# Banded attention and a gated feed-forward on one core: the convolution's weights converted at the start, and the weight chunks converted with two VectorE instructions fewer

## The chip, the cores and the metric

The kernel runs on one core of one Trainium2 chip. The time is the device time of one execution in microseconds (us); before the change it was 523.57 us, the median of three runs (522.38 to 523.83). Five engines work side by side, each through its own list of instructions in a fixed order: TensorE (PE in the profile, its weight loads PEld), VectorE (DVE), ScalarE (ACT), GpSimd (POOL) and SyncE (SP), which here only starts transfers. An instruction at the head of a list that waits holds up everything behind it on that engine.

## What is computed

The reference, cut to what matters:

```python
scores = scale * np.matmul(q, k.transpose(0, 1, 3, 2))     # 8 batches, 8 heads, 576 positions, 64 wide
scores = np.where(masks, scores, -1e9)                      # heads 0-3: last 32 positions; 4-7: every 4th of the last 128
attn = softmax(scores)
x = np.matmul(attn, v)                                      # heads side by side: (8, 576, 512)
h = np.maximum(x @ w_in, 0.0)                               # 512 -> 1024
conv_out = sum(conv_w[k] * shifted(h, k - 1) for k in range(3))
out = (h * sigmoid(conv_out)) @ w_out                       # 1024 -> 512
```

`w_in`, `conv_w` and `w_out` arrive as 64-bit floats, read by the kernel as pairs of 32-bit integers, a low and a high word.

## The kernel before

The matrix products of the feed-forward part are made from pairs: every operand is a high part (rounded to the format `F32R`) plus a low part (what rounding left), and three products (high times high, high times low, low times high) are added in PSUM. So each weight has to be turned from two integer words into such a pair before TensorE can use it, and each attention output `x` too: ScalarE casts the PSUM tile to `x0a`, TensorE subtracts that from the PSUM tile with a matrix `minus` (line 334), and ScalarE casts what is left to `x0b` (line 337).

The work is in tasks. For each of the 8 batches there are 4 attention chains (two heads each: scores on TensorE at line 255, mask and maximum on VectorE at 266 and 268, the exponentials on ScalarE at 275, reciprocal, scaling and a transpose on VectorE at 288, 289 and 291, the values on TensorE at 307), and one expert chain: first product (367), rectifier on ScalarE (374), the convolution's taps, the gate and its split (385 to 396), second product (412), and the store. A planner (`Planner.order`) gets each task with an engine, a cost and a due time from a table (`DUE`), simulates the engines and buffers, and so fixes the order of instructions on every engine. In front of the first products TensorE gets dummy products with the matrix `eye` (`fill`, line 525), as many as fit in what the planner takes for its idle time between 5 and 31.5 us. There are 82 of them, in fixed places of TensorE's order, each a 128x512 product that nothing reads.

There is one PSUM buffer for attention (`att`), two buffers for raw weights (`raw_128` and `raw_129` in the listings), one scratch tile `t`, and two tiles `pt` for transposed probabilities. The weights come in eight chunks of 1 MB, four of `w_in` (converted to tiles `wi`) and four of `w_out` (tiles `wo`). Each chunk takes these steps (lines of the kernel before):

- SP starts the load into `raw` (470);
- ScalarE writes the absolute value of the high words to `t` (476);
- VectorE clamps `t` (477), shifts and masks its bits (479), and puts sign and exponent's top bit back (482): now `t` holds the weight, cut to the bits that `F32R` keeps;
- ScalarE casts `t` to the high part (484);
- VectorE shifts the low words (485) and joins to them the rest of the high words (487), takes the scale from `t` (489), and multiplies both to the low part (491). None of these four waits for ScalarE's cast.

In the order of their conversion, the first chunk goes to `wi_67` (high) and `wi_71` (low), the second to `wi_68` and `wi_72`, the third to `wi_66` and `wi_70`, the fourth to `wi_65` and `wi_69`. The two raw buffers alternate, so the load of the third chunk waits until the first one's last reader is done.

The convolution's 3 x 1024 weights are 24 numbers for each partition (`few_weights`). Their load stands in SP's list behind a dozen others (445); one ScalarE instruction (447) and six on VectorE (448 to 457) make them, as tasks of the planner, and VectorE reads the result `conv_sb` first at line 379.

At the very start, ahead of all tasks, ScalarE starts the load of the mask (497), copies half of the mask table (507 and 509), and makes `minus` and `eye` (499 and 500). TensorE's dummy products need `eye`.

Of the kernel before, what the change touches and what calls it, by code (L numbers as in the profile page):

```python
# [185 lines left out]
def attn_moe(ctx: ExitStack, tc: tile.TileContext, qk_p, qk_d, v_p, v_d, w_in, w_out, conv, mask, out):  # L186
    nc = tc.nc
# [47 lines left out]
    xs = {}  # L235

    def attention(b, p):
# [10 lines left out]
        def scores():  # L248
# [19 lines left out]
        last = plan.add("DVE", 0.755, soft + 0.5, lambda: nc.vector.tensor_reduce(  # L268
            out=m.t, in_=flat(), axis=AX.X, op=ALU.max, negate=slotwise), [last], [s, m])
# [166 lines left out]
    def few_weights(src, due):  # L436

        u, t = few
        low, high = (few_raw[:, :, i] for i in range(2))
        ui, ti = u.bitcast(I32), t.bitcast(I32)  # L440

        def step(run, after, engine="DVE"):
            return plan.add(engine, 0.2, due, run, [after])
# [3 lines left out]
        last = step(lambda: nc.scalar.activation(out=u, in_=high.bitcast(F32), func=AF.Abs), last, "ACT")  # L447
        last = step(lambda: nc.vector.tensor_scalar(out=u, in0=u, scalar1=2.0 ** -15, scalar2=None, op0=ALU.max), last)
        last = step(lambda: nc.vector.tensor_scalar(
            out=ti, in0=ui, scalar1=3, scalar2=0x3fffffff, op0=ALU.logical_shift_left, op1=ALU.bitwise_and), last)  # L450
        last = step(lambda: nc.vector.scalar_tensor_tensor(
            out=ti, in0=high, scalar=-0x40000000, in1=ti, op0=ALU.bitwise_and, op1=ALU.bitwise_or), last)
        last = step(lambda: nc.vector.tensor_scalar(
            out=ui, in0=ti, scalar1=-0x800000, scalar2=None, op0=ALU.bitwise_and), last)
        last = step(lambda: nc.vector.scalar_tensor_tensor(
            out=u, in0=low.bitcast(U32), scalar=2.0 ** -52, in1=u, op0=ALU.mult, op1=ALU.mult), last)
        return step(lambda: nc.vector.tensor_tensor(
            out=conv_sb.rearrange("p t c -> p (t c)"), in0=t, in1=u, op=ALU.add), last)

    def weights(src, due, fetch, hi, lo):  # L460
# [8 lines left out]
        bits = lambda x: x().bitcast(I32)  # L469
        load = plan.add("SP", 3.0, fetch, lambda: nc.sync.dma_start(  # L470
# [124 lines left out]
```

## Time and profile before

| | |
|---|---|
| time, median of three runs | 523.57 us (522.38 to 523.83) |
| the profiled execution | 520.62 us, of which the span from first to last instruction is 518.8 us |
| TensorE busy | 502.6 us (97%) |
| VectorE busy | 389.4 us (75%) |
| ScalarE busy | 303.9 us (59%) |
| granted TensorE clock | 0.999 |

A row of the timeline reads: start (us from the span's start), duration, engine, line, operation, output tile and input tile, shapes, count; in square brackets the engine's idle time ahead of it and what ended that. A row of the windows reads: stretch, its length, then the busy time and number of instructions of PE, PEld, DVE, ACT and POOL, the granted clock, the busy share of the DMA engines and GB/s. Names are of tiles, without their numbers in the timeline and with them in the listings of the order.

### The profile page before, as it was taken

The numbers are of one execution on the slowest core, as the hardware profiler recorded it, in microseconds if no ns is written. First come the engines' busy times: TensorE is split into PE (matmuls) and PEld (weight loads), VectorE is DVE, ScalarE is ACT, GpSimd is POOL, SyncE is SP. The second block draws the span as 40 slices with busy tenths as digits, with TensorE's granted clock in tenths as the row PEclk, the third lists the DMA queues.
The fourth block names the chain that finished last, engine by engine and source line by source line (L and its number), as shares of the span: only waits on it lengthen the run. The fifth ranks groups of instructions, "written<-read, shape, count | busy, mean of one in ns | idle before, by whom it ended". The sixth has DMA issues, their size and how long they took to land.

```text
span 518.8 us, 16673 instructions
## 1 busy us (share of the span) xinstructions
PE 502.6 (97%) x7542; PEld 438.9 (85%) x7542; DVE 389.4 (75%) x552; ACT 303.9 (59%) x624; POOL 1.4 (0%) x27
## 2 busy tenths in 40 slices
PE   5999999999999899999999999999989999999996
PEld 3578999999778898799878997899967899889985
DVE  4999999999986899739970599739989379418800
ACT  5968989748433677158741676448732388327710
POOL 1000000000000000000000000000000000000000
PEclk9999999999999999999999999999999999999999
DMA  7867452211255320413132114321244200110021
GB/s 280 304 200 273 161 158 99 68 52 58 89 178 173 105 80 21 150 52 93 52 103 89 52 48 126 125 82 52 93 119 131 74 1 1 42 42 1 0 62 41
DMA packets 16550, 50.98 MB, mean 98 GB/s; under 512 B 2016, under 2 KB 3168, under 8 KB 15456
## 3 DMA queue, kind: packets, MB, share of 16 engines
q1 hardware_dynamic: 16336, 49.84, 28.7%
q8 instruction: 59, 0.97, 0.8%
q10 hardware_dynamic: 144, 0.08, 0.1%
q14 instruction: 11, 0.09, 0.1%
HBM read 40.48 MB, written 9.44 MB: 96 GB/s over the span
## 4 chain that ended last, share of the span: by engine, by line
PE 86%; DVE 5%; ACT 4%; DMA 4%; issue 1%; ACTq 0%
PE nn L412 37%; PE mm L367 34%; PE att L307 6%; PE att L255 5%; DMA qk<-in_qk_d_dram 2%; PE nn L367 2%; PE nn L525 1%; ACT c L390 1%; ACT L390 1%; DMA c<-in_mask_dram 1%; DMA v<-in_v_p_dram 1%; DVE s L289 1%; DVE pt L291 1%; PE att L334 1%; ACT h L374 0%
## 5 line engine op out<-in xcount | busy, mean ns | idle before, releaser
L412 PE MATMUL nn<-wo,g 128*128 128x512 f32 (+1 forms) x960 | 210.8, 374 | 0.0
L412 PEld LDWEIGHTS nn<-wo,g 128*128 128x128 f32 x960 | 164.6, 188 | 32.0 <-ACT out L422 0.4
L379 DVE SCALAR_TENSOR_TENSOR c<-h,conv_sb,c 128x576 f32<-128x576 f32 x128 | 103.1, 813 | 44.3 <-ACT c L385 43.2
L374 ACT ACTIVATE h<-mm 128x288 f32<-128x288 f32 x120 | 48.3, 407 | 38.3 <-PE mm L367 38.2
L422 ACT COPY out<-nn 128x512 f32<-128x512 f32 (+1 forms) x40 | 21.7, 543 | 62.9 <-PE nn L412 59.0
L367 PE MATMUL mm<-x6a,wi 128*128 128x288 f32 x192 | 54.5, 298 | 0.2 <-ACT h L374 0.2
L392 DVE TENSOR_TENSOR c<-c,h 128x576 f32<-128x576 f32 x64 | 47.6, 755 | 6.8 <-ACT c L390 6.0
L394 ACT CAST g<-c 128x576 fp32r<-128x576 f32 x64 | 42.6, 672 | 17.3 <-DVE c L392 17.2
L385 ACT ACTIVATE c<-h,conv_sb 128x576 f32<-128x576 f32 x64 | 49.6, 777 | 3.7 <-DVE g L396 2.2
L390 ACT ACTIVATE c<-c 128x576 f32<-128x576 f32 x64 | 43.2, 684 | 12.4 <-DVE c L379 11.6
L396 DVE TENSOR_TENSOR g<-c,g 128x576 fp32r<-128x576 f32 x64 | 47.7, 755 | 2.4 <-ACT g L394 1.4
L255 PEld LDWEIGHTS att<-qk 64*32 64x32 f32 x2304 | 26.6, 108 | 18.4 <-issue 5.7
L255 PE MATMUL att<-qk 64*32 64x64 f32 x2304 | 32.2, 229 | 9.7 <-DMA qk<-in_qk_p_dram 5.4
L307 PEld LDWEIGHTS att<-pt,v 32*64 32x64 f32 x2624 | 31.1, 130 | 12.1 <-issue 4.9
L367 PE MATMUL mm<-x3a,wi 128*128 128x288 f32 x144 | 40.8, 299 | 0.2 <-ACT h L374 0.2
L367 PE MATMUL mm<-x2a,wi 128*128 128x288 f32 x144 | 40.8, 299 | 0.0
L367 PE MATMUL mm<-x1a,wi 128*128 128x288 f32 x144 | 40.3, 296 | 0.0
L367 PEld LDWEIGHTS mm<-x6a,wi 128*128 128x128 f32 x192 | 36.1, 188 | 1.0 <-ACT h L374 0.4
L367 PE MATMUL mm<-x5a,wi 128*128 128x288 f32 x128 | 36.4, 299 | 0.2 <-ACT h L374 0.2
L307 PE MATMUL att<-pt,v 32*64 32x64 f32 (+1 forms) x2624 | 34.6, 230 | 1.5 <-ACT x1b L337 1.1
L367 PE MATMUL mm<-x0a,wi 128*128 128x288 f32 x112 | 31.7, 300 | 0.0
L367 PE MATMUL mm<-x6b,wi 128*128 128x288 f32 x96 | 28.4, 296 | 0.0
(122 smaller groups left out, 797.7 us busy)
## 6 DMA issues: line engine op xcount, KB each, us to landing
qk<-in_qk_p_dram SPq DMA_DIRECT2D x16, 592.0 KB, 4.2
qk<-in_qk_d_dram SPq DMA_DIRECT2D x16, 592.0 KB, 4.2
out_dram<-out SPq DMA_DIRECT2D x28, 256.0 KB, 2.2
v<-in_v_d_dram SPq DMA_DIRECT2D x16, 384.0 KB, 3.6
v<-in_v_p_dram SPq DMA_DIRECT2D x16, 384.0 KB, 3.5
raw<-in_w_in_dram SPq DMA_DIRECT2D x4, 1024.0 KB, 6.4
raw<-in_w_out_dram SPq DMA_DIRECT2D x4, 1024.0 KB, 6.6
out_dram<-out SPq DMA_DIRECT2D x16, 128.0 KB, 2.0
```

Of the source, the lines that this page charges most:

```text
L255: nc.tensor.matmul(sc.t[quad * 32:quad * 32 + 32, o:o + W], qk.t[hd * 64:hd * 64 + 64, q0:q0 + 32], qk.t[hd * 64:hd * 64 + 64, S + q0:S + ...
L307: nc.tensor.matmul(tv.t[hd * 64:hd * 64 + 64, o:o + hi - lo], v.t[quad * 32:quad * 32 + 32, i, hd * 64:hd * 64 + 64], pt.t[quad * 32:quad ...
L367: nc.tensor.matmul(ps.t[:, 0:HALF], wi[jw][fc // 2][:, fc % 2, k], x[k].t[jx][:, hf * HALF:hf * HALF + HALF], start=(k == 0 and i == 0), s ...
L374: relu.append(plan.add("ACT", 0.4, due + 1.6 * u + 1.6, lambda fc=fc, hf=hf, ps=ps: nc.scalar.activation(out=h[fc].t[:, 1 + hf * HALF:1 + ...
L379: nc.vector.scalar_tensor_tensor(out=c[fc].t, in0=h[fc].t[:, k:S + k], scalar=conv_sb[:, k, fc:fc + 1], in1=c[fc].t, op0=ALU.mult, op1=ALU ...
L385: t = plan.add("ACT", 0.777, d, lambda fc=fc: nc.scalar.activation(out=c[fc].t, in_=h[fc].t[:, 1:S + 1], func=AF.Copy, scale=conv_sb[:, 1, ...
L390: t = plan.add("ACT", 0.686, d + 1.0, lambda fc=fc: nc.scalar.activation(out=c[fc].t, in_=c[fc].t, func=AF.Sigmoid), [t], [c[fc]], "sigmoid")
L392: t = plan.add("DVE", 0.755, d + 1.5, lambda fc=fc: nc.vector.tensor_tensor(out=c[fc].t, in0=c[fc].t, in1=h[fc].t[:, 1:S + 1], op=ALU.mult ...
L394: hi = plan.add("ACT", 0.675, d + 2.0, lambda fc=fc: nc.scalar.copy(out=half(fc, 0), in_=c[fc].t), [t, *(done[fc] if odd else [])], [c[fc] ...
L396: lo = plan.add("DVE", 0.755, d + 2.5, lambda fc=fc: nc.vector.tensor_tensor(out=half(fc, 1), in0=c[fc].t, in1=half(fc, 0).bitcast(F32), o ...
L412: nc.tensor.matmul(ps.t[:, 0:n], g[k // 2].t[:, k % 2, jg, c0:c0 + 128], w.rearrange("p h c -> p (h c)") if hf is None else w[:, hf], star ...
L422: last = plan.add("ACT", 0.582 if hf is None else 0.37, out_due + 8 * cost * (u + 1), lambda ps=ps, o=o, n=n: nc.scalar.copy(out=o.t[:, 0: ...
```

## The change

It has two parts, and the planner is given the same tasks at the same costs in both, so that its order stays as it was; some tasks now do nothing, and some do something else.

**The convolution's weights.** Their load moves from SP's list to ScalarE's, right behind that of the mask. Their seven instructions leave their places in the order; they are issued by the task of the very first maximum (`greatest`), behind its reduction. The one on ScalarE reads only the load, and there it is placed as soon as ScalarE's own start-up list allows.

**The weight chunks.** The third VectorE step keeps eight more bits of the high word (mask `0x3ffffff8` for `0x3ffff000`). The two steps on the low words do nothing any more. A new step shifts the low words right by 29 and joins them to `t`, so that `raw` holds the weight as a float32 of 24 bits (line 502 of the kernel after). ScalarE's cast of `t` still makes the high part (500), and the low part is now a subtraction, that float32 minus the high part (484), issued by whichever of the two tasks comes second. The task of the cast now counts as a user of the raw buffer. The diff, cut to this:

```diff
+        def greatest():
+            nc.vector.tensor_reduce(out=m.t, in_=flat(), axis=AX.X, op=ALU.max, negate=slotwise)
+            while early:
+                early.pop()()
...
-        last = plan.add("SP", 0.1, due - 2.0, lambda: nc.sync.dma_start(
-            out=few_raw, in_=src.bitcast(I32).rearrange("p (n t) -> p n t", t=2)))
-        last = step(lambda: nc.scalar.activation(out=u, in_=high.bitcast(F32), func=AF.Abs), last, "ACT")
...
+        nc.scalar.dma_start(out=few_raw, in_=src.bitcast(I32).rearrange("p (n t) -> p n t", t=2))
+
+        def steps():
+            nc.scalar.activation(out=u, in_=high.bitcast(F32), func=AF.Abs)
+            nc.vector.tensor_scalar(out=u, in0=u, scalar1=2.0 ** -15, scalar2=None, op0=ALU.max)
...
+        early.append(steps)
+        last = plan.add("SP", 0.1, due - 2.0, lambda: None)
+        for engine in ["ACT"] + 6 * ["DVE"]:
+            last = plan.add(engine, 0.2, due, lambda: None, [last])
...
+        def both(first=None):
+
+            if first:
+                first()
+            come.append(raw.t)
+            if len(come) == 2:
+                nc.vector.tensor_tensor(out=lo, in0=shaped(lw(), lo), in1=hi.bitcast(F32), op=ALU.subtract)
...
-            out=bits(t), in0=bits(t), scalar1=3, scalar2=0x3ffff000,
+            out=bits(t), in0=bits(t), scalar1=3, scalar2=0x3ffffff8,
...
-        high = plan.add("ACT", 1.14, due, lambda: nc.scalar.copy(out=hi, in_=shaped(t(), hi)), [top], [tb])
-        left = step(0.69, [load], lambda: nc.vector.tensor_scalar(
-            out=bits(lw), in0=bits(lw), scalar1=9, scalar2=None, op0=ALU.logical_shift_right))
-        left = step(1.22, [left], lambda: nc.vector.scalar_tensor_tensor(
-            out=bits(lw), in0=bits(hw), scalar=23, in1=bits(lw), op0=ALU.logical_shift_left, op1=ALU.bitwise_or))
-        last = step(0.69, [top, left], lambda: nc.vector.tensor_scalar(
-            out=bits(hw), in0=bits(t), scalar1=-0x800000, scalar2=None, op0=ALU.bitwise_and))
-        return [high, plan.add("DVE", 1.22, due, lambda: nc.vector.scalar_tensor_tensor(
-            out=lo, in0=shaped(lw().bitcast(U32), lo), scalar=2.0 ** -43, in1=shaped(hw(), lo),
-            op0=ALU.mult, op1=ALU.mult), [last], [raw])]
+        high = plan.add("ACT", 1.14, due, lambda: both(lambda: nc.scalar.copy(out=hi, in_=shaped(t(), hi))), [top], [tb, raw])
+        left = step(1.22, [step(0.69, [load], lambda: None)], lambda: None)
+        last = step(0.69, [top, left], lambda: nc.vector.scalar_tensor_tensor(
+            out=bits(lw), in0=bits(lw), scalar=29, in1=bits(t), op0=ALU.logical_shift_right, op1=ALU.bitwise_or))
+        return [high, plan.add("DVE", 1.22, due, both, [last], [raw])]
```

TensorE's order is the same before and after. Three places show what moved on the others. Lines of the kernel after are larger by 2 to 11 than those before for the same instruction.

ScalarE's list at its start, before (`c_123` is the raw mask, `pt_94` holds the unit matrix, `m_88` the first maximum):

```order
L497 DMA c_123<-in_mask_dram 128x320
L507 ACT_TABLE_LOAD
L507 COPY mask_sb<-c_123 128x576
L509 COPY mask_sb<-c_123 128x64
L509 COPY mask_sb<-c_123 128x128
L499 ACTIVATE minus<-pt_94 128x128
L500 CAST eye<-pt_94 128x128
L271 ACTIVATE m_88<-m_88 128x9
```

and after (`few_raw` is the raw convolution weights):

```order
L508 DMA c_123<-in_mask_dram 128x320
L446 DMA few_raw<-in_conv_dram 128x48
L518 ACT_TABLE_LOAD
L518 COPY mask_sb<-c_123 128x576
L449 ACTIVATE few_78<-few_raw 128x24
L520 COPY mask_sb<-c_123 128x64
L520 COPY mask_sb<-c_123 128x128
L510 ACTIVATE minus<-pt_94 128x128
L511 CAST eye<-pt_94 128x128
L276 ACTIVATE m_88<-m_88 128x9
```

The instruction that reads the convolution's weights stands behind the first copy of the mask, with two copies, `minus` and `eye` behind it.

VectorE's list around the first chunk's end, before (`s` and `z` belong to the attention tasks, `pt_95` to the second pair of heads):

```order
L482 SCALAR_TENSOR_TENSOR t_130<-raw_128,t_130 128x1024
L288 RECIPROCAL z_91<-z_91 128x9
L289 TENSOR_TENSOR s_85<-s_85,z_91 128x9x64
L489 TENSOR_SCALAR raw_128<-t_130 128x1024
L491 SCALAR_TENSOR_TENSOR wi_71<-raw_128 128x1024
L291 STREAM_TRANSPOSE pt_95<-s_87 128x576
L288 RECIPROCAL z_92<-z_92 128x9
L289 TENSOR_TENSOR s_86<-s_86,z_92 128x9x64
L485 TENSOR_SCALAR raw_129<-raw_129 128x1024
L487 SCALAR_TENSOR_TENSOR raw_129<-raw_129 128x1024
L477 TENSOR_SCALAR t_130<-t_130 128x1024
```

and after:

```order
L498 SCALAR_TENSOR_TENSOR t_130<-raw_128,t_130 128x1024
L293 RECIPROCAL z_91<-z_91 128x9
L294 TENSOR_TENSOR s_85<-s_85,z_91 128x9x64
L502 SCALAR_TENSOR_TENSOR raw_128<-raw_128,t_130 128x1024
L296 STREAM_TRANSPOSE pt_95<-s_87 128x576
L293 RECIPROCAL z_92<-z_92 128x9
L294 TENSOR_TENSOR s_86<-s_86,z_92 128x9x64
L484 TENSOR_TENSOR wi_71<-raw_128,wi_67 128x1024
L493 TENSOR_SCALAR t_130<-t_130 128x1024
```

The first chunk's last instruction moved behind the next transpose, reciprocal and scaling, and it now reads `wi_67`, which ScalarE's cast writes.

VectorE's list around the fourth chunk's end, before:

```order
L482 SCALAR_TENSOR_TENSOR t_130<-raw_129,t_130 128x1024
L489 TENSOR_SCALAR raw_129<-t_130 128x1024
L491 SCALAR_TENSOR_TENSOR wi_69<-raw_129 128x1024
L288 RECIPROCAL z_91<-z_91 128x9
L289 TENSOR_TENSOR s_85<-s_85,z_91 128x9x64
L291 STREAM_TRANSPOSE pt_94<-s_85 128x576
L266 TENSOR_TENSOR s_86<-att_131,mask_sb 128x9x64
L268 TENSOR_REDUCE m_89<-s_86 128x9
```

and after:

```order
L498 SCALAR_TENSOR_TENSOR t_130<-raw_129,t_130 128x1024
L502 SCALAR_TENSOR_TENSOR raw_129<-raw_129,t_130 128x1024
L484 TENSOR_TENSOR wi_69<-raw_129,wi_65 128x1024
L293 RECIPROCAL z_91<-z_91 128x9
L294 TENSOR_TENSOR s_85<-s_85,z_91 128x9x64
L296 STREAM_TRANSPOSE pt_94<-s_85 128x576
L266 TENSOR_TENSOR s_86<-att_131,mask_sb 128x9x64
L270 TENSOR_REDUCE m_89<-s_86 128x9
```

Here the place is the same; what is new is the read of `wi_65`, the output of ScalarE's cast, with an attention chain's steps in line behind it.

More of the change, by code (lines that the diff above doesn't have):

```diff
@@ L233, in attn_moe @@
              for j in range(2) for c in range(2) for hd in range(2)]
-    xs = {}
+    xs, early = {}, []
     def attention(b, p):
@@ L267, in attention @@
             out=flat(), in0=scored(), in1=masked, op=ALU.add), [last], [sc, s])
-        last = plan.add("DVE", 0.755, soft + 0.5, lambda: nc.vector.tensor_reduce(
-            out=m.t, in_=flat(), axis=AX.X, op=ALU.max, negate=slotwise), [last], [s, m])
+        def greatest():
+            nc.vector.tensor_reduce(out=m.t, in_=flat(), axis=AX.X, op=ALU.max, negate=slotwise)
+            while early:
+                early.pop()()
+        last = plan.add("DVE", 0.755, soft + 0.5, greatest, [last], [s, m])
         if slotwise:
@@ L440, in few_weights @@
         ui, ti = u.bitcast(I32), t.bitcast(I32)
-        def step(run, after, engine="DVE"):
-            return plan.add(engine, 0.2, due, run, [after])
-        last = plan.add("SP", 0.1, due - 2.0, lambda: nc.sync.dma_start(
-            out=few_raw, in_=src.bitcast(I32).rearrange("p (n t) -> p n t", t=2)))
-        last = step(lambda: nc.scalar.activation(out=u, in_=high.bitcast(F32), func=AF.Abs), last, "ACT")
-        last = step(lambda: nc.vector.tensor_scalar(out=u, in0=u, scalar1=2.0 ** -15, scalar2=None, op0=ALU.max), last)
@@ L449, in few_weights @@
[L449 to L456, printed above, removed]
@@ L457, in few_weights @@
-        return step(lambda: nc.vector.tensor_tensor(
-            out=conv_sb.rearrange("p t c -> p (t c)"), in0=t, in1=u, op=ALU.add), last)
+        nc.scalar.dma_start(out=few_raw, in_=src.bitcast(I32).rearrange("p (n t) -> p n t", t=2))
+        def steps():
+            nc.scalar.activation(out=u, in_=high.bitcast(F32), func=AF.Abs)
+            nc.vector.tensor_scalar(out=u, in0=u, scalar1=2.0 ** -15, scalar2=None, op0=ALU.max)
+            nc.vector.tensor_scalar(out=ti, in0=ui, scalar1=3, scalar2=0x3fffffff, op0=ALU.logical_shift_left,
+                                    op1=ALU.bitwise_and)
+            nc.vector.scalar_tensor_tensor(out=ti, in0=high, scalar=-0x40000000, in1=ti, op0=ALU.bitwise_and,
+                                           op1=ALU.bitwise_or)
+            nc.vector.tensor_scalar(out=ui, in0=ti, scalar1=-0x800000, scalar2=None, op0=ALU.bitwise_and)
+            nc.vector.scalar_tensor_tensor(out=u, in0=low.bitcast(U32), scalar=2.0 ** -52, in1=u, op0=ALU.mult,
+                                           op1=ALU.mult)
+            nc.vector.tensor_tensor(out=conv_sb.rearrange("p t c -> p (t c)"), in0=t, in1=u, op=ALU.add)
@@ L460, in weights @@
+        early.append(steps)
+        last = plan.add("SP", 0.1, due - 2.0, lambda: None)
+        for engine in ["ACT"] + 6 * ["DVE"]:
+            last = plan.add(engine, 0.2, due, lambda: None, [last])
+        return last
     def weights(src, due, fetch, hi, lo):
@@ L469, in weights @@
         bits = lambda x: x().bitcast(I32)
+        come = []
+        def both(first=None):
[4 more added lines that the diff above has]
+                nc.vector.tensor_tensor(out=lo, in0=shaped(lw(), lo), in1=hi.bitcast(F32), op=ALU.subtract)
         load = plan.add("SP", 3.0, fetch, lambda: nc.sync.dma_start(
```

## The prediction

> **What bounds the kernel now.** I read the page's first part, then the windows, and then the timelines of the first 90 us engine by engine. The span and the busy times:
>
> ```profile
> span 518.8 us, 16673 instructions
> PE 502.6 (97%) x7542; PEld 438.9 (85%) x7542; DVE 389.4 (75%) x552; ACT 303.9 (59%) x624; POOL 1.4 (0%) x27
> ```
>
> The windows of four stages (length, then busy time of PE, PEld, DVE, ACT, POOL):
>
> ```profile
> 7.14:33.70 26.56, 26.56 (x554) 15.25 (x554) 24.08 (x36) 22.58 (x108) 0.00 (x0) 1.00 0.79 279
> 35.03:61.70 26.67, 25.59 (x598) 24.18 (x599) 25.41 (x39) 22.69 (x82) 0.00 (x0) 1.00 0.64 234
> 61.70:130.00 68.30, 68.30 (x869) 65.89 (x869) 66.69 (x88) 50.90 (x90) 0.00 (x0) 1.00 0.25 83
> 130.00:510.00 380.00, 375.87 (x5434) 328.98 (x5433) 270.89 (x388) 203.00 (x338) 0.00 (x0) 1.00 0.24 76
> ```
>
> TensorE never pauses from 7.14 to 33.7 us, nor from 61.7 to 130, and from 130 to 510 it pauses 4.13 us in 380. It does a fixed list in a fixed order, so whatever makes it later by the time of 90 us makes the end later by as much, and the same holds for a gain. Three places in TensorE's timeline matter:
>
> ```profile
> 7.14 1.46 PE L525 MATMUL nn<-eye 128*128 128x512 bf16 x3 [0.41 <-ACT eye L500]
> 35.03 1.07 PE L307 MATMUL att<-pt,v 32*64 32x32 f32 x80 [1.14 <-ACT x1b L337]
> 36.92 0.84 PE L334 MATMUL att<-x2a,minus 128*128 128x144 f32 x6
> ```
>
> The dummy products start when ScalarE has made `eye`; since they have no slack until 33.7 us, a later `eye` moves all of that stage, though the work is useless. The pause of 1.14 us ahead of 35.03 is the only large one that a faster VectorE could close: there the second chunk's steps on VectorE hold up a cast on ScalarE, with `x1b` behind it.
>
> **Part one, the convolution's weights.** ScalarE's copies at the start, the old place of the ScalarE instruction, and VectorE's pause behind the first maximum:
>
> ```profile
> 6.24 0.44 ACT L509 COPY mask_sb<-c 128x64 bf16<-128x64 bf16 x2
> 29.60 0.21 ACT L447 ACTIVATE few<-few_raw 128x24 f32<-128x24 f32 x1
> 9.79 0.76 DVE L266 TENSOR_TENSOR s<-att,mask_sb 128x576 f32<-128x576 f32 x1 [1.48 <-PE att L255]
> ```
>
> On VectorE six instructions of about 0.21 us (none is longer than ScalarE's here) are 1.3 us, and the pause behind the first maximum is 1.48 us: nothing. Their old place, near 36 us, gave VectorE's list 1.3 us, but there TensorE waits for ScalarE; nothing gained either. SP's list loses one small load, and one load of queries now stands ahead of the sixth chunk's instead of behind it, which starts later: nothing.
>
> On ScalarE the instruction now stands ahead of the copies of 6.24, so they, `minus`, `eye` and the dummy products wait for the load of the convolution's weights. It is started right behind the mask's, on the same queue (q10). The mask's landing, and the packets in 2.4:3.8 (the first pair) and in 3.8:5.1:
>
> ```profile
> c<-in_mask_dram ACTq DMA_DIRECT2D x1, 80.0 KB, 4.8
> q1 hardware_dynamic: 78, 0.37, 72.8%
> q10 hardware_dynamic: 71, 0.05, 14.9%
> q1 hardware_dynamic: 121, 0.50, 95.4%
> q10 hardware_dynamic: 73, 0.04, 9.5%
> ```
>
> The mask is 144 packets, 9 for each of 16 engines, and while both queues hold work they go about one for one with SP's (71 beside 78). The convolution's load has as many rows, 128, so I take 144 packets too. In 1.3 us 194 packets passed, 12 an engine, 0.107 us each; nine pairs are 1.9 us. From the mask's end, 5.1 us, that is 7.0, and with the 0.4 us from the mask's last packet to its landing (0.7 + 4.8 = 5.5) it is 7.4. With 0.15 us for the instruction itself, between the nothing of a covered start and its 0.21 us, the copies start at 7.55 for 6.24: **TensorE 1.3 us late**. Bounds: 0.15 if the load is there by 6.24, and 2.1 if it goes at the mask's own pace (144 packets from 2.4 to 5.1). I take the later half's pace, since the early packets ran while the first loads were starting.
>
> The Trainium skill, page "DMA: Bandwidth & Descriptors", section "Queues, rings and completion order", says that a DMA engine alternates between its queues by whole packets of typically 9 to 17 descriptors; by that the nine small rows would follow the mask's at once, and the delay would be the lower bound. The one-for-one counts above speak against it.
>
> **Part two, the first three chunks.** The four steps that go, and a subtraction of the same kind as the new one:
>
> ```profile
> 28.82 0.69 DVE L485 TENSOR_SCALAR raw<-raw 128x1024 int32<-128x1024 int32 x1
> 29.55 1.23 DVE L487 SCALAR_TENSOR_TENSOR raw<-raw 128x1024 int32<-128x1024 int32 x1
> 25.38 0.69 DVE L489 TENSOR_SCALAR raw<-t 128x1024 int32<-128x1024 int32 x1
> 26.10 1.23 DVE L491 SCALAR_TENSOR_TENSOR wi<-raw 128x1024 fp32r<-128x1024 uint32 x1
> L396 DVE TENSOR_TENSOR g<-c,g 128x576 fp32r<-128x576 f32 x64 | 47.7, 755 | 2.4 <-ACT g L394 1.4
> ```
>
> For 3.84 us come a two-tile step of 1.23 (as L487) and the subtraction. By the 0.755 us for 576 elements it is at most 1.34 us for 1024, and by L491, two tiles and 1024 elements, 1.23; I take 1.22. Each chunk saves VectorE 1.4 us, 11 us over eight. But the subtraction reads the cast's output, which the old last step did not:
>
> ```profile
> 27.45 1.05 ACT L484 CAST wi<-t 128x1024 fp32r<-128x1024 f32 x1
> 27.36 1.16 SPq L470 DMA_DIRECT2D raw<-in_w_in_dram  x1
> raw<-in_w_in_dram SPq DMA_DIRECT2D x1, 1024.0 KB, 6.3
> raw<-in_w_in_dram SPq DMA_DIRECT2D x1, 1024.0 KB, 4.8
> 34.88 1.19 ACT L476 ACTIVATE t<-raw 128x1024 f32<-128x1024 f32 x1
> 36.14 0.64 ACT L330 CAST x2a<-att 128x576 fp32r<-128x576 f32 x1
> ```
>
> The cast ends at 28.50, behind `x0a`, which is paced by the dummy products: 29.8 with the 1.3. The subtraction ends at 31.0, and only then is `raw_128` free: the third chunk's load starts at 31.0 instead of 27.36. It lands 4.8 us later (the fourth chunk's, which found the queue nearly empty; 6.3 is the third's, behind another load), at 35.8. ScalarE's `Abs` on it, until 37.0, stands ahead of `x2a`, which starts at 37.0 for 36.14. Line 334 had 0.14 us of slack (36.92 against 36.78), so **TensorE is 0.75 us late there**. The second chunk's saving makes `x1b` ready earlier, and this gives back 0.55 of the 1.3, no more: the load ends last. With 6.3 us it would be 2.25 late.
>
> **The fourth and sixth chunk.** Here VectorE, with less work, arrives early and waits for the cast, with attention steps behind it:
>
> ```profile
> 52.52 1.22 DVE L491 SCALAR_TENSOR_TENSOR wi<-raw 128x1024 fp32r<-128x1024 uint32 x1
> 53.13 1.04 ACT L484 CAST wi<-t 128x1024 fp32r<-128x1024 f32 x1
> 54.69 0.78 DVE L291 STREAM_TRANSPOSE pt<-s 128x576 f32<-128x576 f32 x1
> 56.15 0.75 DVE L268 TENSOR_REDUCE m<-s 128x9 f32<-128x576 f32 x1
> 56.94 0.21 ACT L271 ACTIVATE m<-m 128x9 f32<-128x9 f32 x1 [0.15 <-DVE m L268]
> 60.43 0.62 ACT L330 CAST x4a<-att 128x576 fp32r<-128x576 f32 x1
> 56.57 1.06 PE L307 MATMUL att<-pt,v 32*64 32x32 f32 x80
> 61.66 0.84 PE L334 MATMUL att<-x4a,minus 128*128 128x144 f32 x6
> ```
>
> The cast ends at 54.17, or 54.9 with 0.75; the subtraction at 56.15, where the old step ended at 53.74: VectorE is 2.4 us late. The transpose then ends at 57.9, and the values (L307) wanted it at 57.3: 0.6 more. The maximum ends at 59.3, so the chain of ScalarE from 56.94 to `x4a` is 2.4 late, `x4a` ends at 63.45, and line 334 wanted it at 63.0: 0.5 more. TensorE is 1.85 late.
>
> ```profile
> 71.19 1.23 DVE L491 SCALAR_TENSOR_TENSOR wo<-raw 128x1024 fp32r<-128x1024 uint32 x1
> 71.20 1.05 ACT L484 CAST wo<-t 128x1024 fp32r<-128x1024 f32 x1
> 86.69 0.75 DVE L396 TENSOR_TENSOR g<-c,g 128x576 fp32r<-128x576 f32 x1
> 87.28 3.89 PE L412 MATMUL nn<-wo,g 128*128 128x256 f32 x30
> ```
>
> In the sixth chunk the step that ended at 72.42 becomes a subtraction from 72.25 to 73.5, 1.05 late. VectorE's list then has no pause until the `g` that ends at 87.44, which TensorE reads at once; a removed 0.69 (L485) in between leaves 0.4. **In all 0.75 + 0.6 + 0.5 + 0.4 = 2.25 us slower.** Behind that, VectorE is ahead and TensorE's pauses are few.
>
> The profiled execution took 520.62 us (its span plus 1.8), 2.95 less than the median; it would take 522.9. The median becomes 523.57 + 2.25 = **525.8**. About 0.3%, 1.57 us, is what a measurement of this kernel can tell from no change, so slower begins at 525.14.
>
> **Rivals.**
>
> 1. *The load is there in time* (the page's rule on turns; it needs a landing by 6.24). TensorE's first delay is 0.15, the third load lands at 34.65, and `x2a` starts at 35.85, 0.3 early instead of late; the 1.5 us of the fourth and sixth chunk remain: 1.5 - 0.3 = 1.2, 524.8. For it: the rows are small. Against: the one-for-one counts.
> 2. *The third load takes 6.3 us*: 1.5 more, 527.3. For it: this load itself took 6.3. Against: its queue is nearly empty by then.
> 3. *Faster*: the load in time, and ScalarE's casts early enough that no subtraction waits. Then VectorE's saving closes TensorE's pause of 1.14 us: 522.4; with the half of it 523.0. It decides if ScalarE reaches its casts at least 1.2 us earlier than now, at 53.13 and at 71.20. Against: both casts stand behind work that TensorE paces. To be faster by over 1.57 us, it would need more than that pause.
>
> **Chances.** The forecast 0.45 (524.9 to 527.0; 0.05 of it within 0.3%), the first rival 0.25, the second 0.15, the third 0.15 (0.05 of it beyond 0.3%). So slower 0.55, same 0.40, faster 0.05. The range runs from 523.0, half-way into the third rival, to 527.8, the second with its delay of `eye` somewhat larger, and leaves out less than 0.2.
>
> **What would show it.** Right: the first dummy product at about 8.4 us, the idle time ahead of ScalarE's second copy put down to the load of the convolution's weights; the third chunk's load started near 31 us, and `x2a` near 37; VectorE idle ahead of the fourth chunk's subtraction, put down to the cast. Wrong: dummy products still at 7.2 to 7.3 us, or TensorE's second products (L412) starting at 87.3 or earlier.

## The result and the profile after

The kernel after took 524.73 us (median of 20 runs, 523.53 to 529.09); the kernel before, run beside it, 521.63 us (20 runs, 519.58 to 523.86). The ratio is 1.0074, with a 95% interval of 1.0058 to 1.0089: of 521.63 us that is 3.9 us slower, 3.0 to 4.6. The forecast was 2.25 us slower, in the right direction and too small. That 524.73 is nonetheless below the forecast's 525.8 comes from its base: the three runs of 523.57 lay 1.94 above the median of twenty. A base too high and a step too small partly cancel, so that the two times lie close together by luck. The ratios compare undisturbed runs alone and aren't the quotients of the medians given beside them (here 1.0059, or 3.1 us, near the lower end of the interval). The runs after scatter more than those before: seven of the twenty took 526.34 us or more, and neither profile of this kernel shows such a run.

The section on the kernel before counts 82 dummy products. There are 78: its profile has 7542 products, that of the kernel without dummy products, further down, 7464.

The profiled execution after took 523.63 us, against 520.62 before. Its page:

```profile
span 521.6 us, 16671 instructions
PE 504.6 (97%) x7542; PEld 439.3 (84%) x7542; DVE 380.3 (73%) x536; ACT 304.0 (58%) x624; POOL 1.4 (0%) x27
```

VectorE has 9.1 us less to do (389.4 before), and the span is 2.8 us longer. The rest of this section goes through the prediction's places, in order of time.

**The start.** ScalarE's timeline, one load from the part on transfers, and TensorE's timeline, all of the kernel after:

```profile
7.29 0.22 ACT L449 ACTIVATE few<-few_raw 128x24 f32<-128x24 f32 x1 [1.20 <-DMA few_raw<-in_conv_dram]
7.42 0.42 ACT L520 COPY mask_sb<-c 128x64 bf16<-128x64 bf16 x2
1.17 0.45 ACTq L446 DMA_DIRECT2D few_raw<-in_conv_dram  x1
few_raw<-in_conv_dram ACTq DMA_DIRECT2D x1, 24.0 KB, 6.1
8.30 1.46 PE L536 MATMUL nn<-eye 128*128 128x512 bf16 x3 [1.68 <-ACT eye L511]
9.70 1.33 PE L255 MATMUL att<-qk 64*32 64x64 f32 x72
10.96 4.64 PE L536 MATMUL nn<-eye 128*128 128x512 bf16 x18
15.53 0.97 PE L255 MATMUL att<-qk 64*32 64x64 f32 x72
```

The load of the convolution's weights was issued at 1.17 and landed 6.1 us later, at 7.27; ScalarE stood idle for it for 1.20 us, the copies began at 7.42 for 6.24, and the dummy products at 8.30 for 7.14. The second scores are 1.17 us late (9.70 for 8.53), the third 1.86 (15.53 for 13.67): between them the same 18 dummy products took 4.64 us for 4.06.

**The third chunk.** VectorE's first subtraction, SP's issue, the load's duration, ScalarE and TensorE, after:

```profile
30.40 1.23 DVE L484 TENSOR_TENSOR wi<-raw,wi 128x1024 fp32r<-128x1024 f32 x1
31.65 0.33 SPq L486 DMA_DIRECT2D raw<-in_w_in_dram  x1
raw<-in_w_in_dram SPq DMA_DIRECT2D x1, 1024.0 KB, 4.9
36.64 1.17 ACT L492 ACTIVATE t<-raw 128x1024 f32<-128x1024 f32 x1 [0.72 <-DMA raw<-in_w_in_dram]
37.69 0.64 ACT L335 CAST x2a<-att 128x576 fp32r<-128x576 f32 x1
35.98 1.07 PE L312 MATMUL att<-pt,v 32*64 32x32 f32 x80 [0.21 <-ACT x1b L342]
38.39 0.93 PE L339 MATMUL att<-x2a,minus 128*128 128x144 f32 x6 [0.36 <-ACT x2a L335]
```

The load is issued when the subtraction ends (30.40 + 1.23 = 31.63), lands at 31.65 + 4.9 = 36.55, and ScalarE waits 0.72 us for it. The pause ahead of the third values has shrunk from 1.14 to 0.21, so that they are only 0.95 late (35.98 for 35.03). Ahead of the subtraction of `x2a` is a new pause, 0.36, and the place is 1.47 late (38.39 for 36.92).

**The fourth chunk.** ScalarE's cast, VectorE and TensorE, after:

```profile
54.68 1.03 ACT L500 CAST wi<-t 128x1024 fp32r<-128x1024 f32 x1
55.74 1.23 DVE L484 TENSOR_TENSOR wi<-raw,wi 128x1024 fp32r<-128x1024 f32 x1 [2.17 <-ACT wi L500]
57.92 0.78 DVE L296 STREAM_TRANSPOSE pt<-s 128x576 f32<-128x576 f32 x1
58.63 0.72 DVE L266 TENSOR_TENSOR s<-att,mask_sb 128x576 f32<-128x576 f32 x1
55.14 0.96 PE L255 MATMUL att<-qk 64*32 64x64 f32 x72 [0.44 <-DMA qk<-in_qk_d_dram]
59.40 1.07 PE L312 MATMUL att<-pt,v 32*64 32x32 f32 x80 [1.11 <-DVE s L266]
```

VectorE waits 2.17 us for the cast, as foreseen. TensorE's fourth values then wait 1.11 us. But they wait for line 266, not for the transpose: the transpose ends at 58.70, and the mask's addition, which empties the one PSUM buffer `att`, at 59.35. From scores to values TensorE loses 1.18 us (55.14 for 53.49 is 1.65; 59.40 for 56.57 is 2.83). The subtraction of `x4a` costs nothing more (64.47 for 61.66 is 2.81).

**The sixth chunk.** VectorE, ScalarE and TensorE, after:

```profile
75.26 1.23 DVE L484 TENSOR_TENSOR wo<-raw,wo 128x1024 fp32r<-128x1024 f32 x1 [0.76 <-ACT wo L500]
78.27 3.25 DVE L384 SCALAR_TENSOR_TENSOR c<-h,conv_sb,c 128x576 f32<-128x576 f32 x4
81.56 0.69 ACT L395 ACTIVATE c<-c 128x576 f32<-128x576 f32 x1 [0.56 <-DVE c L384]
82.15 0.39 ACT L379 ACTIVATE h<-mm 128x288 f32<-128x288 f32 x1
82.59 0.40 PE L372 MATMUL mm<-x6a,wi 128*128 128x288 f32 x1 [0.26 <-ACT h L379]
87.95 0.40 PE L372 MATMUL mm<-x6a,wi 128*128 128x288 f32 x1 [0.16 <-ACT h L379]
91.25 0.94 PE L417 MATMUL nn<-wo,g 128*128 128x256 f32 x5
```

The same taps on VectorE (384 here, 379 there) in the kernel before:

```profile
74.20 3.25 DVE L379 SCALAR_TENSOR_TENSOR c<-h,conv_sb,c 128x576 f32<-128x576 f32 x4
```

The subtraction waits 0.76 us for the cast. Behind it VectorE's taps come late (78.27 for 74.20, 1.1 us more than TensorE's 2.99), ScalarE waits 0.56 us for one of them, and behind that stands the rectifier (379), which ends at 82.54 and frees a PSUM buffer `mm` that TensorE wants for a first product. Matched start by start with the kernel before, TensorE goes from 2.99 late to 3.52 behind the pause at 82.59, to 3.68 behind 85.94 and to 3.95 at 87.95. The second products start at 91.25 for 87.28: 3.97 late.

**Behind it.** The next large pause, in the kernel before: SP's issue of a query load, its duration, and the scores that read it:

```profile
165.28 0.33 SPq L243 DMA_DIRECT2D qk<-in_qk_p_dram  x1
qk<-in_qk_p_dram SPq DMA_DIRECT2D x1, 592.0 KB, 5.6
171.04 0.96 PE L255 MATMUL att<-qk 64*32 64x64 f32 x72 [1.61 <-DVE pt L291]
```

and after:

```profile
169.26 0.33 SPq L243 DMA_DIRECT2D qk<-in_qk_p_dram  x1
qk<-in_qk_p_dram SPq DMA_DIRECT2D x1, 592.0 KB, 4.2
173.63 0.96 PE L255 MATMUL att<-qk 64*32 64x64 f32 x72 [0.23 <-DMA qk<-in_qk_p_dram]
```

In the kernel before the load landed at 165.28 + 5.6 = 170.9, just ahead of 171.04: I read the 1.61 us as a wait for that transfer, although the row names VectorE, whose transpose ended at 171.00: in the last profile below the same scores start at 167.62, ahead of that transpose at 168.48. In this execution of the kernel after the transfer took 4.2 us and the pause was 0.23. That takes 3.97 down to 2.59, and is why the two spans differ by 2.8 us and not by 4.

### The profile page after: what moved, and what is told of

Its sections match the earlier page's. It is cut to its first block, busy times and chain, and to the rows that moved or that the text cites. A ratio compares the mean times of both kernels' runs of the same rounds, so it can differ in the third digit from the quotient of the medians.

```text
span 521.6 us, 16671 instructions
## 1 busy us (share of the span) xinstructions
PE 504.6 (97%) x7542; PEld 439.3 (84%) x7542; DVE 380.3 (73%) x536; ACT 304.0 (58%) x624; POOL 1.4 (0%) x27
## 4 chain that ended last, share of the span: by engine, by line
PE 83%; ACT 7%; DVE 4%; DMA 4%; issue 1%; ACTq 0%
PE nn L417 37%; PE mm L372 31%; PE att L312 6%; PE att L255 5%; PE nn L536 3%; ACT s L280 1%; DVE c L384 1%; DMA few_raw<-in_conv_dram 1%; ACT c L395 1%; ACT L395 1%; ACT h L379 1%; DMA raw<-in_w_in_dram 1%; PE nn L372 1%; DVE c L397 1%; DMA qk<-in_qk_p_dram 1%
## 5 line engine op out<-in xcount | busy, mean ns | idle before, releaser
L266 DVE TENSOR_TENSOR s<-att,mask_sb 128x576 f32<-128x576 f32 x32 | 24.1, 752 | 8.3 <-PE att L255 8.3
```

The source lines that it names most:

```text
L266: last = plan.add("DVE", 0.75, soft + 0.0, lambda: nc.vector.tensor_tensor(out=flat(), in0=scored(), in1=masked, op=ALU.add), [last], [sc, s])
```

## The experiments

The theory is the prediction's: a late `eye`, a third load that waits for the subtraction, and the waits for the cast in the fourth and sixth chunk. Rivals: the loss comes from the convolution's part alone, or from the chunks alone, or it is the scatter of the start. The table gives, for each kernel, how much later (or earlier) TensorE is than in the kernel before over one stretch: the start of the same instruction at the stretch's end minus that in the profile of before, less the same difference at its beginning. Marks are times in the kernel before.

| stretch of TensorE | after | after again | conv. alone | chunks alone | conv. behind `eye` | old 4, 6 | old 1, 3, 4, 6 | before again |
|---|---|---|---|---|---|---|---|---|
| first dummy product (7.14) | +1.16 | +1.86 | +1.30 | -0.09 | +0.14 | +0.06 | -0.12 | -0.13 |
| 2nd to 3rd scores (8.53 to 13.67) | +0.69 | +0.53 | +0.74 | +0.75 | +1.17 | +0.01 | +1.10 | +0.43 |
| third values to `x2a` (35.03 to 36.92) | +0.52 | +0.72 | +0.01 | +0.51 | +0.86 | +0.65 | +0.29 | +0.01 |
| fourth chunk (53.49 to 56.57) | +1.18 | +0.98 | 0.00 | +1.72 | +1.28 | +0.01 | 0.00 | 0.00 |
| sixth chunk (71.40 to 87.28) | +0.98 | +0.97 | -0.02 | +0.97 | +0.98 | +0.23 | +0.22 | -0.01 |
| second products (87.28), in all | +3.97 | +4.68 | +3.03 | +2.68 | +5.51 | +0.53 | +0.91 | +1.07 |

### The convolution's part alone

The kernel after with the chunks' steps of the kernel before:

```diff
-        high = plan.add("ACT", 1.14, due, lambda: both(lambda: nc.scalar.copy(out=hi, in_=shaped(t(), hi))), [top], [tb, raw])
...
+        left = step(0.69, [load], lambda: nc.vector.tensor_scalar(
+            out=bits(lw), in0=bits(lw), scalar1=9, scalar2=None, op0=ALU.logical_shift_right))
...
```

> Part one alone: the convolution's weights early, the weight chunks converted as before. Positions of TensorE's instructions against the kernel before: second scores 8.53, third scores 13.67, third values 35.03, second products 87.28. Theory A (a late eye costs its own delay plus a slow start of the dummy products, and VectorE's list, which is dense from 17 us on, passes it all through): second scores +1.2, third scores +1.9, third values +1.9, second products +1.9, time +1.5 to 2.0 us. Rival B (the delay of useless work is soaked up by the pauses behind it, and the whole loss comes from the chunks): third scores +1.9, third values below +1.0, second products within 0.3, time within 0.5 us.

It took 523.42 us against 520.83, ratio 1.0055 (1.0027 to 1.0084). TensorE's timeline:

```profile
8.44 1.46 PE L531 MATMUL nn<-eye 128*128 128x512 bf16 x3 [1.60 <-ACT eye L506]
56.55 0.96 PE L255 MATMUL att<-qk 64*32 64x64 f32 x72 [1.23 <-DMA qk<-in_qk_d_dram]
59.63 1.07 PE L312 MATMUL att<-pt,v 32*64 32x32 f32 x80
```

The first dummy product is late (8.44), the fourth values wait for nothing, and the table's three stretches of the chunks are as in the kernel before. So this part costs by itself, and in this profile at the start; with VectorE's list as full as before, nothing is given back at the third values, which are 2.06 late. VectorE's six instructions add nothing there: they run from 8.33 to 9.58, and VectorE then waits 1.62 us for the next scores. The rest of the 3.03, which is over the 1.9 expected, is a query load that holds TensorE for 1.23 us ahead of 56.55 (0.35 in the kernel before).

### The chunks' part alone

The kernel before with the new steps:

```diff
+            if len(come) == 2:
+                nc.vector.tensor_tensor(out=lo, in0=shaped(lw(), lo), in1=hi.bitcast(F32), op=ALU.subtract)
...
-        left = step(1.22, [left], lambda: nc.vector.scalar_tensor_tensor(
-            out=bits(lw), in0=bits(hw), scalar=23, in1=bits(lw), op0=ALU.logical_shift_left, op1=ALU.bitwise_or))
...
```

> Part two alone: new conversion of all chunks, the convolution's weights as before. Theory A: second and third scores as before, third values 1.0 earlier (34.0), x2a's subtraction (36.92) about 0.3 earlier because the third load is started only at 29.9 and ends last, fourth values (56.57) +0.8, second products (87.28) +1.7; time +1.3 to 2.0 us. Rival B (the loss is all the chunks'): second products +3 to +4. Rival C (without the late eye, ScalarE is early enough for its casts and VectorE's 11 us saved count): fourth values not later than before, second products 0 to 1 us earlier.

It took 522.93 us against 520.83, ratio 1.0036 (1.0015 to 1.0057). SP's issue of the third chunk, and TensorE:

```profile
30.47 0.33 SPq L480 DMA_DIRECT2D raw<-in_w_in_dram  x1
58.13 1.06 PE L307 MATMUL att<-pt,v 32*64 32x32 f32 x80 [1.18 <-DVE s L266]
```

The third load is late here too (30.47), the first dummy product is in time, and the steps of the fourth and sixth chunk are there. The second products are 2.68 late where 1.7 was expected; 0.75 of it is the stretch of slow dummy products ahead of the third scores. The two parts together would be 1.0091; 1.0074 was measured for both, within the intervals. Neither part is a gain.

### The convolution's steps behind `eye`

The kernel after, with the seven instructions issued behind ScalarE's first scaling instead of by the task of the maximum:

```diff
-            while early:
-                early.pop()()
...
+            def scaled():
+                nc.scalar.mul(out=m.t, in_=m.t, mul=SCALE)
+                while early:
+                    early.pop()()
```

> The changed kernel with ScalarE's instruction on the convolution's weights moved behind the copies, minus, eye and the first scaling of a maximum; its load stays where the change put it. Theory A: dummy products start as before (7.1 to 7.2), third scores within 0.1 of 13.67, second products +1.7 to 2.0 against the kernel before and 2.0 lower than in the changed kernel; time 1.5 to 2.2 us under the changed kernel. Rival B (the delay of eye costs nothing in the end): second products as in the changed kernel, 91.2, and the same time.

It took 525.29 us, ratio 1.0091 (1.0059 to 1.0123), so the gain expected from it did not show. TensorE's timeline:

```profile
7.28 1.46 PE L539 MATMUL nn<-eye 128*128 128x512 bf16 x3 [0.41 <-ACT eye L514]
9.94 5.12 PE L539 MATMUL nn<-eye 128*128 128x512 bf16 x18
56.59 1.33 PE L255 MATMUL att<-qk 64*32 64x64 f32 x72 [2.21 <-DMA qk<-in_qk_d_dram]
```

The dummy products do start in time (7.28), and the steps of the chunks are as in the kernel after. But 18 dummy products took 5.12 us here, and a query load, 8.6 us from issue to landing, held TensorE for 2.21. Both also vary between executions of unchanged kernels, and this is one profile alone. The times point the same way, though: all four runs (523.82 to 527.21 us) lie above all five of the chunks' part alone (521.35 to 523.65), so the convolution's part seems to cost something even where `eye` is in time, and what that is stays open. That the new place brings a gain is not shown.

### The old steps in the fourth and sixth chunk

The kernel before with the new steps in the other six chunks:

```diff
-    converted = lambda c, src, pair: weights(src, WEIGHTS[c], FETCH[c], *pair)
+    converted = lambda c, src, pair: (weights_old if c in (0, 5) else weights)(src, WEIGHTS[c], FETCH[c], *pair)
```

> Part two alone, but the fourth and the sixth chunk converted by the old four steps, which wait for no cast. Theory A (VectorE waiting for the cast with attention and gate steps behind it is the loss there): fourth values and the subtraction for x4a 0.2 to 0.4 earlier than before, second products 0 to 0.4 earlier than before, time 0.2 to 0.5 us under the kernel before. Rival D (what delays the fourth values is the later transfers behind a raw buffer that is freed later, or any lateness of ScalarE, not the wait): fourth values +0.5 to +1.1 as in e2, second products +1 or more.

It took 521.41 us against 520.83, ratio 1.0002 (0.9973 to 1.0031). TensorE's timeline:

```profile
34.17 1.07 PE L307 MATMUL att<-pt,v 32*64 32x32 f32 x80 [0.22 <-ACT x1b L337]
36.71 0.93 PE L334 MATMUL att<-x2a,minus 128*128 128x144 f32 x6 [0.48 <-ACT x2a L330]
56.69 1.07 PE L307 MATMUL att<-pt,v 32*64 32x32 f32 x80
```

The step of the fourth chunk is gone, that of the sixth is down from 0.97 to 0.23, so the wait for the cast is the cause of both. At the second products the loss of the chunks' part falls from 2.68 to 0.53; 0.74 of that fall is the scatter of the slow dummy products. The two ratios agree with that, but their intervals overlap, and the gain of 0.2 to 0.5 us that was expected did not show. The start was undisturbed in this execution, so it shows best what the first chunks do: VectorE's saving brings the third values 0.86 us ahead of 35.03, and the pause for `x2a` (0.48), where the third load comes late, leaves 0.21 at 36.92.

### Before and after once more

> The kernel before, a second trace, to see which of the differences between the traces are the execution's own. Theory A: the dummy products between second and third scores run slowly for a time that differs from execution to execution (third scores 5.1 to 5.9 us after the second; in the first trace of before 5.14), the transfer of queries ahead of the scores at 53.49 and the one ahead of the scores at 171.04 land up to 2 us apart between executions, and all other distances on TensorE repeat within 0.1 us. Rival B: they are the kernel's own, and this trace repeats 5.14, a pause of 0.35 at 53.5 and one of 1.6 at 171 within 0.2.

> The changed kernel, a second trace. Theory A: the first dummy product 1.1 to 1.3 us later than in the kernel before, ScalarE idle for 1.2 us ahead of its second copy, VectorE waiting 2.0 to 2.5 us for the cast of the fourth chunk, fourth values 1.1 to 1.3 us further behind than the scores ahead of them, 1.0 us more from the last values of the first batch to the second products; only the dummy products' slow stretch and the two transfers of queries differ. Rival B: one of these distances differs by more than 0.3 us from the first trace.

One execution of each: before 521.64 us, after 525.15. ScalarE's start in the latter:

```profile
7.99 0.22 ACT L449 ACTIVATE few<-few_raw 128x24 f32<-128x24 f32 x1 [1.45 <-DMA few_raw<-in_conv_dram]
```

The wait for the convolution's load is there again, longer, and the first dummy product is 1.86 late, beyond the 1.1 to 1.3 expected. The steps of the three chunks repeat within 0.2 us, and are zero in the kernel before. The stretch between the second and third scores does not repeat: 5.14 us in the first profile of before, 5.57 in the second. Over the kernels whose `eye` is late it is 5.83, 5.67 and 5.88, over the others 5.14, 5.57, 5.89, 6.31, 5.15 and 6.24: means of 5.79 and 5.72. So the 0.69 us of the kernel after in that stretch can't be put down to the change.

### The kernel after with fewer dummy products

The filler leaves 0.8 us of each gap free instead of 0.3, which makes 60 dummy products of 78:

```diff
-        for t in plan.filled(plan.order(), fill, 5.0, 31.5, 0.22, 0.3):
+        for t in plan.filled(plan.order(), fill, 5.0, 31.5, 0.22, 0.8):
```

> The changed kernel with 18 of its 78 dummy products left out (each row of them shorter by 2 or 3). Theory A (the late eye costs time only because the dummy products fill TensorE's list without slack): third scores near 14.0 instead of 15.5, fourth chunk and sixth chunk cost as before, second products near 89 instead of 91.2, time 1.5 to 2.5 us under the changed kernel. Rival B (fewer dummy products leave TensorE slow for longer, or ScalarE's chain sets the pace): third scores 14.8 or later, second products 90.5 or later.

It took 522.71 us against 521.28, ratio 1.0032 (1.0012 to 1.0052). The second scores start at 8.81 (9.70 in the kernel after) although `eye` is as late, the third values at 34.95 (35.98), the second products at 90.55 (91.25). That looks as if the loss at the start were paid through the dummy products, but the kernel before gains as much by the same cut (further down: third values 0.90 earlier, second products 0.92). Against it, with 60 in both, the kernel after is 4.19 late at the second products (90.55 for 86.36), where it was 3.97 late with 78. The third scores came at 14.79 and the second products at 90.55, close to what the rival named (14.8 and 90.5 or later), not near 14.0 and 89. So fewer dummy products make either kernel faster and don't soak up the cost of the change; the steps of the fourth and sixth chunk remain (1.25 and 0.98).

### The old steps in the first, third, fourth and sixth chunk

As above, with `c in (0, 1, 2, 5)`.

> Convolution's weights as before, new steps only in the second, fifth, seventh and eighth chunk. Theory A (the third load is late because the first chunk's raw buffer is freed behind the cast): third load started at 27.4, third values 0.9 earlier than before, no pause ahead of the subtraction for x2a, which comes 0.8 to 0.9 earlier, fourth values and second products 0.6 to 0.9 earlier than before, transfers aside; time 0.5 to 0.9 us under the kernel before. Rival B (x2a waits for something else than the load): the subtraction for x2a no more than 0.3 earlier, as in e4, and no gain in the end.

It took 521.75 us against 521.28, ratio 1.0012 (0.9988 to 1.0036). SP's issue of the third chunk, its duration, ScalarE and TensorE:

```profile
28.35 1.59 SPq L510 DMA_DIRECT2D raw<-in_w_in_dram  x1
raw<-in_w_in_dram SPq DMA_DIRECT2D x1, 1024.0 KB, 7.0
35.50 1.16 ACT L516 ACTIVATE t<-raw 128x1024 f32<-128x1024 f32 x1 [0.50 <-DMA raw<-in_w_in_dram]
37.24 0.93 PE L334 MATMUL att<-x2a,minus 128*128 128x144 f32 x6
```

With the first chunk by the old steps the third load is issued 2.1 us earlier than with the chunks' part alone (30.47), so the new subtraction does hold its issue back. But issued right behind another load it took 7.0 us, and it landed at 35.35; 30.47 + 4.9 is 35.37. ScalarE waits for it here as well, and TensorE's step is down to 0.29 from 0.51, not gone. So the late issue is only a part of that loss. For the rest I take it that the second chunk's saving takes away the pause ahead of it: what was hidden behind that pause now ends last. That is argued from the rows; no run tests it alone. The gain of 0.5 to 0.9 us that was expected fell too: with 78 dummy products, no mix of old and new steps was faster than the kernel before.

### The kernel before with fewer dummy products

The experiment on the kernel after pointed to this one: 60 dummy products in the kernel before, and in the version with the old steps in the fourth and sixth chunk.

> The kernel before with 60 dummy products instead of 78 (the filler leaves 0.8 us of each gap free instead of 0.3). Theory (VectorE's list, not the dummies, sets the start of the third values, line 307, in the kernel before: there TensorE pauses 1.14 us for a cast that stands behind VectorE's second chunk): TensorE reaches that place up to 1 us earlier and waits longer for it; the third values start 0 to 0.3 us earlier than 35.03, the second products (line 412) 0 to 0.3 earlier than 87.28, ratio to before 0.999 to 1.000. Rival (the dummies take time from real work all the way, and 18 fewer of them at 0.22 us give much of their 4 us back): second products 0.7 us or more earlier, ratio 0.9985 or less. Second rival (with fewer of them TensorE's products run slow for longer): ratio above 1.001.

> The kernel before with the new low part in chunks 1, 2, 3, 5, 7 and 8 (chunks 4 and 6 by the old steps), and with 60 dummy products instead of 78. Theory: VectorE is 1.4 us a chunk lighter in the first three, so that here an earlier TensorE is not held by the pause of 1.14 us; the third chunk's load is freed by work that the dummies pace, and starts about 0.7 us earlier than with 78. The third values start 1.0 to 1.5 us earlier than 35.03, the second products at 86.6 to 87.1 (0.7 to 1.2 earlier than with 78 dummies), ratio to before 0.9980 to 0.9990. Rival (dummies cost nothing, TensorE waits for the third load whatever stands ahead): second products at 87.5 or later, ratio 1.000.

The kernel before took 517.64 us against 521.36: ratio 0.9933 (0.9913 to 0.9954). The other took 519.11: 0.9965 (0.9951 to 0.9980). For the first of them my theory fell and the first rival held. VectorE's timeline in the kernel before:

```profile
16.97 0.76 DVE L266 TENSOR_TENSOR s<-att,mask_sb 128x576 f32<-128x576 f32 x1 [0.42 <-PE att L255]
```

and with 60 dummy products VectorE's and TensorE's:

```profile
16.05 0.76 DVE L266 TENSOR_TENSOR s<-att,mask_sb 128x576 f32<-128x576 f32 x1 [0.15 <-PE att L255]
31.24 1.23 DVE L482 SCALAR_TENSOR_TENSOR t<-raw,t 128x1024 int32<-128x1024 int32 x1
34.13 1.07 PE L307 MATMUL att<-pt,v 32*64 32x32 f32 x80 [0.60 <-ACT x1b L337]
```

I had held that VectorE's list sets the start of the third values, and it does. But that list waits at 16.97 for scores which stand behind dummy products on TensorE. With fewer it goes on at 16.05, everything on it comes 0.9 us earlier (31.24 for 32.14), and so do the third values (34.13). In the second version the third values came at 33.91 and the second products at 86.74, as expected, and the ratio lower than expected (0.9980 to 0.9990). It still waits 0.42 us at `x2a`, and by the times it is the slower of the two.

### No dummy products, and 60 once more

The first has `5.0, 5.0` for `5.0, 31.5` in the line of the filler; the second is an unchanged copy.

> The kernel before without any dummy product. Theory (each dummy delays real work behind it on TensorE, and through later scores VectorE's list as well): TensorE is earlier again than with 60, but from 8 to 31 us it then waits for loads and casts; third values (line 307) 0.9 to 1.6 us ahead of 35.03, second products (line 412) at 85.7 to 86.5, ratio to before 0.990 to 0.995. Rival (the dummies hold TensorE's rate up: without them the real products of the first 35 us run at half rate): a group of 72 score products takes 1.3 us instead of 0.96 beyond 13 us, third values 0.3 us earlier at most, ratio 0.997 or more.

> The kernel before with 60 dummy products once more. Its first profile showed 0.9 us less at the second products, while its times were 3.7 us under those of the kernel before, and that profiled execution was the slowest of its six. If the rest is early too (shorter slow stretch at the start, or less waiting for query transfers near 53, 153 and 171 us), this profile shows third values 1.5 us or more ahead of 35.03, or one of those waits gone; if the gain of the times is smaller on this chip, the ratio is 0.996 to 0.998 and the profile is as the first.

Without any, 519.69 us against 521.08: ratio 0.9975 (0.9956 to 0.9995), slower than with 60. TensorE:

```profile
15.13 1.33 PE L255 MATMUL att<-qk 64*32 64x64 f32 x72 [2.53 <-DVE s L266]
```

Here my theory fell, and the rival held: a group of 72 score products takes 1.33 us at 15.13, where it took 0.97 at 15.53 in the kernel after, and the third values are 0.96 late (35.99). The dummy products do hold TensorE's rate up; 78 were only more than it takes.

With 60 again the times repeat: 518.20 us, ratio 0.9931 (0.9911 to 0.9952). This profile, the fastest of its runs (516.80 us, span 515.0), has the third values 0.75 us early, not the 1.5 named, and the second products 1.11 early. The pause ahead of 171.04 (1.61 us, and 1.57 in the first profile with 60) isn't there, and behind it TensorE is 3.41 us early, 3.81 at the end. In the first profile with 60 it was only 0.13 early behind that place and 1.09 at the end. Of the 3.5 us that the runs show, about 1 us has a place that both traces show and that the dummy products explain. Where the rest lies is open: it may be in pauses for query loads, which change from one execution to the next.

## Why the prediction was right, and where it was not

**The late `eye`: right.** Forecast 1.3 us, measured 1.17 at the second scores; landing 7.27 for 7.4. The estimate from packets going one for one held, as the kernel after shows in 5.1:6.3, where q10 carries the convolution's load:

```profile
q1 hardware_dynamic: 101, 0.51, 103.6%
q10 hardware_dynamic: 94, 0.02, 7.1%
```

The Trainium skill, page "DMA: Bandwidth & Descriptors", section "Queues, rings and completion order", has an engine drain a whole packet, typically 9 to 17 descriptors, before it turns to another queue; these counts speak against such turns. That the small load would follow the mask's at once is the prediction's own reading: the section doesn't say it, and by its rule a packet of SP's queue may go between. The load was not there by 6.24 in either execution of the kernel after (waits of 1.20 and 1.45 us), and the first rival falls with it. What this delay costs at the end is less sure: with `eye` in time, the kernel after was no faster (ratio 1.0091).

**Given back at the third values: too small.** 0.55 was allowed for, 0.91 came (1.86 late at the third scores, 0.95 at the third values): VectorE's saving closed nearly all of the pause of 1.14. It paid once, and the third load then took over, as the prediction said.

**The third load: right, on a later base.** Forecast: issued at 31.0, `x2a` cast at 37.0, TensorE 0.75 late. Measured: 31.65, 37.69 and 1.47. The difference of 0.65 to 0.72 fits the 0.69 of the slower dummy products, which the prediction did not have and which the repeats don't tie to the change; it reaches this place because the list ahead of the cast is paced by those products. (The forecast's own rows give 0.72 for its 0.75: 0.86 late, less 0.14 of slack.) The load took 4.9 us (4.8 forecast, 6.3 in the second rival, which falls). What the prediction put down to the late issue alone is only partly that: issued early, the same load lands hardly sooner.

**The fourth chunk: the sum right, the route not.** 0.6 at the values and 0.5 at `x4a` were forecast; 1.18 came at the values and nothing at `x4a`. The step that failed is "The transpose then ends at 57.9, and the values (L307) wanted it at 57.3": the values also need the one PSUM buffer `att`, which the mask's addition behind the transpose on VectorE has to empty. Having waited there, TensorE was no longer early at `x4a`. That 1.1 and 1.18 agree is luck.

**The sixth chunk: mis-sized.** Forecast 0.4, measured 0.98, and the same in each of five profiles with the new step (0.97 to 0.98). The step that failed is "VectorE's list then has no pause until the `g` that ends at 87.44". That is so of VectorE's list, but I followed VectorE to its last reader and did not look at ScalarE's list, where the rectifier stands behind work that waits for VectorE's taps. The removed 0.69 that was to leave 0.4 (L485, at 80.81 in the kernel before) stands behind the first of these taps, too late to help. TensorE was stopped there three times, 0.53, 0.16 and 0.27 us, before `g` mattered. With the old step it falls to 0.23, so that the wait is shown as the cause; the route rests on the rows of ScalarE above.

**In all** 0.75 + 1.1 + 0.4 = 2.25 were forecast; 1.47 + 1.18 + 0.98 = 3.63 were found at these places, 0.69 of it the scatter of the dummy products, and 0.34 in small steps between them. The third rival, faster, had its condition at neither cast: at 54.68 and 74.19 they came later than before, not 1.2 us earlier. And 9.1 us less work on VectorE bought nothing lasting, since TensorE is busy for 97% of the span and only one of its pauses was VectorE's.

## What to carry to other kernels

When a cheaper form of a step reads the result of another engine that the old form didn't need, the saving is the small part: look at what stands behind that instruction on its own engine, at which buffer its inputs now hold, and follow every engine that waits for it, not only the last reader. An instruction placed early because "the engine is free there" still puts all behind it on its own list under its load. Filler work on a busy engine delays real work through the engines that wait for it; count it as work, and size it by trial.

## What the runs showed of the hardware

- The first dummy products run slow for a time that changes from one execution to the next: 18 of them took 4.06 us (before), 4.64 (after) and 5.12 (convolution behind `eye`), while the granted clock of the windows reads 1.00. The Trainium skill, page "TensorE: Matmul & The Clock Gate", section "What's actually happening", says that TensorE starts at half rate and is released after a window of some 3.4 us that runs on its own. The scatter and, without dummy products, the 1.33 us for a group of 72 scores at 15.13 agree with that; the gate itself isn't seen in these traces.
- The same query load of 592 KB took 5.6 us from issue to landing in the kernel before and 4.2 after (read near 171 us), and TensorE's pause ahead of the scores at 53.49 was anything from nothing to 2.21 us over these kernels, 0.35 and 0.57 in two executions of the kernel before. This moves a single execution by as much as a step of this change.
- While both had work, the packets of SP's queue and of ScalarE's passed about one for one: 78 beside 71 in the kernel before (2.4:3.8), 101 beside 94 in the kernel after (5.1:6.3).
- A load of 1 MB took 7.0 us when it was issued 0.48 us behind another load, and 4.9 when it was issued 2.9 us behind it, so the earlier issue landed no sooner.
- Products overlap (0.29 us each, one every 0.13), and the first behind a pause takes 0.40, with the next 0.24 behind it: the pause shown as 0.26 at 82.59 makes what follows 0.53 late.
